# Keys times values of two neighbouring pairs of heads as one group of matmuls, and the queries' 576 columns divided 288 + 288

## The chip, the cores and the metric

The kernel runs on one core of one Trainium2 chip. Its time is the device time of one execution in microseconds (us). The kernel before took 711.76 us, the median of three runs (710.95 to 711.96).

## The reference

Linear attention over 8 batches, 8 heads, 576 positions and 64 dimensions, and then a feed-forward layer with the maximum of three products:

```python
q_s = np.exp(q - np.max(q, axis=-1, keepdims=True))
q_s = q_s / (np.sum(q_s, axis=-1, keepdims=True) + 1e-09)
k_s = np.exp(k - np.max(k, axis=2, keepdims=True))
k_s = k_s / (np.sum(k_s, axis=2, keepdims=True) + 1e-09)
kv = np.einsum('bhsd,bhse->bhde', k_s, v)
attn = np.einsum('bhsd,bhde->bhse', q_s, kv)
x = attn.transpose(0, 2, 1, 3).reshape(4608, 512)
h = np.maximum(np.maximum(x @ w1, x @ w2), x @ w3)   # w1..w3: 512 x 768
return h @ w_out                                     # 768 x 512
```

## The kernel before

**What is computed where.** The heads are worked on in pairs: 8 batches of 4 pairs are 32 pairs, numbered n = 4b + g, and a pair's 2 x 64 dimensions fill the 128 partitions. The feed-forward layer runs over nine chunks of 512 rows: chunk c below 8 holds the first 512 positions of batch c, and the ninth the last 64 positions of all eight batches (the tile `left`). Its products are made exact enough by splitting each operand into a high and a low part in the 32-bit format fp32r: x and the weights each become two tiles, and three matmuls (low weight by high x, high weight by low x, high by high) take the place of one. A gate's matmul (L775, into `pf`) and one of the second layer (L814, also `pf`) each stream 512 columns, with a weight load of 128 x 128 for each. "Wide matmul" stands for one of these below. There are 2592 of them.

**The attention of a pair.** The first two batches (8 pairs, "turned" in the code) go another way, which the change leaves alone. The other 24 pairs ("plain") run so:

- keys: the maximum over the positions by three DVE operations (L486 to L488) and a partition reduction on POOL (L491), then the subtraction on DVE (L494, into `ke`), then the exponential on ACT (L501). The tile `ke` has two buffers.
- keys times values (L519): ten matmuls of 65 columns (64 of the values and one of ones, which gives the sum), five slices of positions by two heads, each head into its own half of the partitions of `sm`. They are plain fp32, and the trace shows two matmul records for each. `sm` has one PSUM bank.
- normalization: 1/sum on DVE (L530, L531), the scaled product rounded to fp32r on ACT (L535, `bdh`) and the rest of it on DVE (L539, `bdl`), both as matrices of 128 x 128 with the heads' blocks on the diagonal.
- queries: softmax on DVE and ACT, then a transpose in blocks on DVE (L613, `tb`), eight DMAs on SP that put the blocks in place (L626, `qT`), and the split into `q_h` (ACT, L632) and `q_l` (DVE, L635).
- queries times keys-values (L690): three fp32r products (`bdh` by `q_l`, `bdl` by `q_h`, `bdh` by `q_h`) over 576 columns. Since a PSUM bank holds 512, each product is one matmul of 512 columns into `pa` and one of 64 into `sm`. `pa` has three banks, `pf` four.
- x: ACT rounds the result to its high part (L693 for the 512 columns, L700 for the 64), DVE subtracts for the low part (L695, L702).

**What sets the order.** Nothing is ordered by hand here: a planner (`Streams`) takes every piece of work as a `Step` with an engine, an estimated cost, what it waits for (`after`), the buffers that it takes and frees, and a rank. It issues the step that can begin first by its own clocks, and at equal time the one with the lowest rank. TensorE's gates and second-layer matmuls have the highest ranks and so fill what is left between the steps of the attention. The result is one fixed order for each engine; an engine works through its list in order, and waits on semaphores. SP's list holds all loads and the `qT` and output DMAs.

Of the kernel before, what the change touches and what calls it, by code (L numbers as in the profile page):

```python
# [43 lines left out]
BANKS = 3, 1  # L44

Q_BY_ACT = (0, 3, 4, 5, 6, 7)

Q_AFTER = (1,)


def dve(n):
    return (n + 90) / 960
# [150 lines left out]
def linear_attention_then_maxout_ffn(  # L203
# [63 lines left out]
    vbuf = [const.tile([P, 2, 5, NV], F32, name=f"vt{i}") for i in range(2)]  # L267
    bdh, bdl = [], []
    early = early_stack.enter_context(tc.tile_pool(name="early", bufs=1))
# [25 lines left out]
    nc.gpsimd.memset(bdf, 0.0)  # L295

    def main_rows(src, b, hs):
        return src[b, hs, 0:CH].rearrange("h (p s) d -> p h s d", s=4)
# [8 lines left out]
    for c in range(B + 1):  # L307
        in_pf += [(c, j, i) for j in range(NJ) for i in range(3)] + [(c, "y", t) for t in range(4)]
    st = Streams({"pf": 4, "pa": BANKS[0], "sm": BANKS[1], "keT": 1, "hp": NJ, "tmp": 3, "ke": 2, "qe": 2, "qf": 1, "qt": 2, "tb": 1, "qT": 2, "qhl": 1}, {"pf": in_pf})
    late_pools, turn_pools = [], []  # L310
# [67 lines left out]
    class Pair:  # L378


        def __init__(self, b, g):
            self.b, self.g = b, g
            self.hs = slice(2 * g, 2 * g + 2)
            self.n = b * NP + g
            self.m = self.n % 2
            self.turned = b < TURNED
            if b == 0:
                self.kt, self.vt, self.qt = k0[:, :, self.hs], v0[:, self.hs], q0[:, self.hs]
            else:
                self.kt, self.vt = kbuf[self.m], vbuf[self.m]  # L390
# [5 lines left out]
        def ago(self, what, *u):  # L396

            return (what, self.n - 2, *u) if self.n >= 2 else None

# [22 lines left out]
        def v_load(self):  # L422
            if self.b:
                prev = self.ago("kv") if self.n >= NP + 2 else None
# [55 lines left out]
        def k_plain(self):  # L480
# [10 lines left out]
            nc.gpsimd.partition_all_reduce(kma, km, P, bass_isa.ReduceOp.max)  # L491
            yield Step("V", dve(640), take=[("ke", n)], gives=("ksub", n), port="V")
            ke = self.ke = att.tile([P, 5, 2, D], F32, name="ke")
            nc.vector.tensor_tensor(  # L494
# [4 lines left out]
            )  # L499
            yield Step("A", act(640))  # L500
            nc.scalar.activation(out=ke, in_=ke, func=AF.Exp)  # L501

        def k_steps(self):
            n, turned = self.n, self.turned
            yield from self.k_turned() if turned else self.k_plain()
            ke = self.ke
            after = turned and n in Q_AFTER
            yield Step(
                "T", 0.9, [("v", n), None if turned else self.ago("xmm")], take=() if turned else [self.small_room()],
                free=[("ke", n)], gives=("kv", n),  # L510
            )
            if not turned:
                self.take_small()
            kv = self.sm[:, 2 * P : 3 * P]
            nv = D if turned else NV
            for s in range(5):
                rows = slice(0, LEFT if turned and s == 4 else P)
                for hh, r in enumerate(heads):
                    nc.tensor.matmul(  # L519
                        out=kv[r, :nv], lhsT=ke[rows, s, hh, :], rhs=self.vt[rows, hh, s, 0:nv],  # L520
                        start=(s == 0), stop=(s == 4),
                    )
            yield Step("V", 0.35)
            rk = att.tile([P, 1], F32, name="rk", bufs=4)
            if turned:
                nc.vector.tensor_scalar(
                    out=rk, in0=self.ks[:, 0:1], scalar1=self.ks[:, 1:2], scalar2=1e-9, op0=ALU.add, op1=ALU.add
                )
            else:
                nc.vector.tensor_scalar_add(out=rk, in0=kv[:, D:NV], scalar1=1e-9)  # L530
            nc.vector.reciprocal(out=rk, in_=rk)  # L531
            yield Step("A", 0.65, free=[self.small_room()] if turned and not after else (), gives=("bd", n) if turned else None)
            for r in heads:
                to = bdf[:, n] if turned else bdh[self.m]
                nc.scalar.activation(out=to[r, r], in_=kv[r, 0:D], func=AF.Copy, scale=rk[r])  # L535
            if not turned:
                yield Step("V", 0.45, gives=("bd", n))
                for r in heads:
                    nc.vector.scalar_tensor_tensor(  # L539
                        out=bdl[self.m][r, r],  # L540
                        in0=kv[r, 0:D],
                        scalar=rk[r],
                        in1=bdh[self.m][r, r].bitcast(F32),
                        op0=ALU.mult,
                        op1=ALU.subtract,
                    )


        def q_steps(self):
# [66 lines left out]
            for i in range(P // BL):  # L616
                for e in range(2):
                    end = i == P // BL - 1 and e == 1
                    yield Step(
                        "S", 0.6, take=[("qT", n)] if i == e == 0 else (), free=[("tb", n)] if end else (),  # L620
                        gives=("qT", n) if end else None, kb=36,
                    )
                    if i == e == 0:
# [4 lines left out]
                        in_=tb[BL * i : BL * (i + 1), e, :],  # L628
                    )
            yield Step("A", act(S), [("qT", n)], take=[("qhl", n)])  # L630
            q_h = turn_pools[0].tile([P, S], F32R, name="q_h", bufs=1)
# [38 lines left out]
        def x_steps(self):  # L670
            n, b = self.n, self.b
            room = ("pa", ("x", n))
            after_sums = self.turned and n in Q_AFTER
            cost = 0.5 if after_sums else f32(CH) if self.turned else 3 * f32r(CH) + 0.2
            freed = ("qe", ("xn", n)) if after_sums else ("qf" if self.turned else "qhl", n)
            after = [("bd", n), ("qhl", n), ("gates", b - 2) if b >= 2 else None, "late" if b == 1 else None]
            yield Step("T", cost, after, take=[room], gives=("xmm", n), free=[freed])
            xT = pa.tile([P, CH], F32, name="pa")
# [12 lines left out]
            h, lo = (xbuf[b % 2][:, i, self.g, :] for i in range(2))  # L691
            yield Step("A", act(CH))
            nc.scalar.copy(out=h, in_=xT)  # L693
            yield Step("V", dve(CH), free=[room], gives=("x", b, self.g))
            nc.vector.tensor_sub(out=lo, in0=xT, in1=h.bitcast(F32))  # L695
            if self.turned:
                return
            h, lo = (left[:, i, self.g, b * LEFT : (b + 1) * LEFT] for i in range(2))
            yield Step("A", act(LEFT))
            nc.scalar.copy(out=h, in_=self.sm[:, 0:LEFT])  # L700
            yield Step("V", dve(LEFT), free=[self.small_room()], gives=("xl", b, self.g))
            nc.vector.tensor_sub(out=lo, in0=self.sm[:, 0:LEFT], in1=h.bitcast(F32))  # L702

# [196 lines left out]
    def open_turn():  # L900
        yield Step("-", 0.0, [("split", n) for n in range(NS)] + [("x", 1, g) for g in range(NP)], gives="turn")
        start_stack.close()
        turn_pools.append(ctx.enter_context(tc.tile_pool(name="turn", bufs=1, side="right", reuse_waits="tile")))
        for i in range(2):
            nc.gpsimd.memset(kbuf[i][LEFT:P, :, 4, :], LOWEST)
            nc.gpsimd.memset(vbuf[i][:, :, :, D:NV], 1.0)
            nc.gpsimd.memset(vbuf[i][LEFT:P, :, 4, :], 0.0)
        for name, to in (("bdh", bdh), ("bdl", bdl)):
            for i in range(2):
                to.append(turn_pools[0].tile([P, P], F32R, name=f"{name}{i}"))  # L910
                nc.gpsimd.memset(to[i].bitcast(F32), 0.0)
# [97 lines left out]
```

## Time and profile before

| | |
|---|---|
| median of three runs | 711.76 us |
| profiled execution, first to last instruction | 711.8 us |
| wide matmuls of the gates (L775), on the chain | 63% of the span |
| wide matmuls of the second layer (L814), on the chain | 21% |
| keys times values (L519 into `sm`), on the chain | 3.0% |
| queries times keys-values (L690), on the chain | 3.6% into `pa`, 0.3% into `sm` |
| DVE, ACT, POOL busy | 56%, 34%, 8% |

In rows of a timeline the columns are the start (us), how long the instruction lasted (us), the engine, the line, the operation, what it writes and reads, and its shape; in square brackets stands the idle time of its engine just before it. PE is TensorE's matmul side and PEld its weight loads. A matmul's recorded length runs past the start of the next one, because matmuls are pipelined; what a matmul costs is read from one start to the next.

### The profile page before, as it was taken

To read this page: it belongs to the slowest core of one execution; us is meant where nothing else is said; L and a number is where in the kernel's file an instruction comes from. 1 tells how busy PE (TensorE), PEld (TensorE's weight loads), DVE (VectorE), ACT (ScalarE), POOL (GpSimd) and SP (SyncE) were. 2 spreads that over 40 slices of the span, in tenths; PEclk is the share of its full clock that TensorE was granted. 3 is DMA by queue.
4 is the path that set the end of the run, shared out by engine and by line. 5 is a ranking of instruction groups with operands and counts; after the bars stand their busy time and mean duration, and the time that the engine had idled before them with its cause. 6 is when DMAs were issued, how large, how long until landed. Compare 5 with 4: busy or idle time off the path is not lost.

```text
span 711.8 us, 9805 instructions
## 1 busy us (share of the span) xinstructions
PE 681.8 (96%) x3542; PEld 553.5 (78%) x3542; DVE 400.0 (56%) x804; ACT 245.0 (34%) x554; POOL 56.3 (8%) x71
## 2 busy tenths in 40 slices
PE   3579999999999999999999999999999999999997
PEld 2367777788887888888888888888888888888886
DVE  5679988789789775865576547643432112211220
ACT  5479867334343324312442134223321111111111
POOL 3223232200010001000000000000000000000000
PEclk9779999999999999999999999999999999999999
DMA  9747523344363215420342035302200010010002
GB/s 222 207 134 232 169 93 106 110 105 113 80 175 103 62 41 154 122 51 17 106 134 73 16 95 135 82 0 72 72 2 0 16 45 0 1 45 15 1 0 60
DMA packets 83280, 58.06 MB, mean 82 GB/s; under 512 B 49184, under 2 KB 74784, under 8 KB 83232
## 3 DMA queue, kind: packets, MB, share of 16 engines
q1 hardware_dynamic: 83152, 57.31, 28.9%
q8 instruction: 28, 0.46, 0.3%
q14 instruction: 20, 0.16, 0.1%
q10 hardware_dynamic: 80, 0.13, 0.0%
HBM read 40.89 MB, written 9.44 MB: 71 GB/s over the span
## 4 chain that ended last, share of the span: by engine, by line
PE 92%; DMA 3%; SPq 2%; DVE 1%; ACT 0%; issue 0%; ACTq 0%; DVEq 0%
PE pf L775 63%; PE pf L814 21%; PE pa L690 4%; DMA wst<-in_moe_w_dram 3%; PE sm L519 3%; SPq L870 0%; SPq L413 0%; PE sm L690 0%; PE pa L645 0%; PE pa L453 0%; PE pa L744 0%; SPq L873 0%; DVE qm L559 0%; DVE wl L374 0%; PE pa L472 0%
## 5 line engine op out<-in xcount | busy, mean ns | idle before, releaser
L775 PE MATMUL pf<-x,wh 128*128 128x512 f32 x1152 | 356.8, 391 | 0.0
L775 PEld LDWEIGHTS pf<-x,wh 128*128 128x128 f32 x1152 | 216.7, 188 | 45.2 <-issue 0.2
L775 PE MATMUL pf<-x,wl 128*128 128x512 f32 x576 | 229.8, 399 | 0.7 <-ACT bdf L535 0.7
L787 DVE TENSOR_TENSOR m<-pf,m 128x512 f32<-128x512 f32 x108 | 74.6, 690 | 179.0 <-PE pf L775 174.6
L775 PEld LDWEIGHTS pf<-x,wl 128*128 128x128 f32 x576 | 108.2, 188 | 25.3 <-ACT bdf L535 0.9
L790 ACT CAST h_h<-m 128x512 fp32r<-128x512 f32 x54 | 33.5, 621 | 201.5 <-DVE m L787 201.5
L814 PE MATMUL pf<-ol,h_h 128*128 128x512 f32 x216 | 88.1, 408 | 0.0
L814 PE MATMUL pf<-oh,h_l 128*128 128x512 f32 x216 | 84.4, 391 | 0.0
L814 PE MATMUL pf<-oh,h_h 128*128 128x512 f32 x216 | 84.1, 389 | 0.0
L784 ACT COPY m<-pf 128x512 f32<-128x512 f32 x54 | 31.6, 586 | 59.4 <-PE pf L775 59.1
L814 PEld LDWEIGHTS pf<-ol,h_h 128*128 128x128 f32 x216 | 40.5, 188 | 9.4 <-issue 0.7
L814 PEld LDWEIGHTS pf<-oh,h_l 128*128 128x128 f32 x216 | 40.5, 188 | 9.0
L794 DVE TENSOR_TENSOR h_l<-m,h_h 128x512 fp32r<-128x512 f32 x54 | 37.0, 686 | 18.0 <-ACT h_h L790 17.9
L814 PEld LDWEIGHTS pf<-oh,h_h 128*128 128x128 f32 x216 | 40.6, 188 | 8.4 <-issue 0.7
L491 POOL PARTITION_ALL_REDUCE kma<-km x24 | 17.3, 722 | 347.4 <-DVE ke L494 281.2
L775 PE MATMUL pf<-left,wh 128*128 128x512 f32 x144 | 44.4, 389 | 0.0
L832 ACT COPY m<-pf 128x512 f32<-128x512 f32 x35 | 20.5, 587 | 55.2 <-PE pf L814 54.9
L359 POOL TENSOR_TENSOR wst<-wx,wst 128x512 int32<-128x512 int32 x24 | 31.3, 1305 | 90.1 <-DVE wx L355 58.8
L695 DVE TENSOR_TENSOR x<-pa,x 128x512 fp32r<-128x512 f32 x32 | 22.0, 688 | 26.9 <-ACT x L693 26.8
L693 ACT CAST x<-pa 128x512 fp32r<-128x512 f32 x32 | 18.7, 584 | 39.5 <-PE sm L690 33.9
L775 PEld LDWEIGHTS pf<-left,wh 128*128 128x128 f32 x144 | 27.0, 188 | 5.7
L613 DVE STREAM_TRANSPOSE tb<-qt 128x576 f32<-128x576 f32 x24 | 30.6, 1275 | 1.2 <-DMA qT<-tb 0.9
(143 smaller groups left out, 675.3 us busy)
## 6 DMA issues: line engine op xcount, KB each, us to landing
wst<-in_moe_w_dram SPq DMA_DIRECT2D x18, 512.0 KB, 5.4
out_dram<-m SPq DMA_DIRECT2D x32, 256.0 KB, 2.5
vt<-in_v_dram SPq DMA_DIRECT2D x56, 128.0 KB, 3.0
qt<-in_q_dram SPq DMA_DIRECT2D x24, 288.0 KB, 3.1
qT<-tb SPq DMA_DIRECT2D x192, 36.0 KB, 1.9
kt<-in_k_dram SPq DMA_DIRECT2D x24, 256.0 KB, 3.1
wst<-in_moe_w_out_dram SPq DMA_DIRECT2D x6, 512.0 KB, 3.5
q<-in_q_dram SPq DMA_DIRECT2D x8, 256.0 KB, 6.0
```

Of the source, the lines that this page charges most:

```text
L359: nc.gpsimd.tensor_add(out=low.bitcast(I32), in0=x.bitcast(I32), in1=low.bitcast(I32))
L519: nc.tensor.matmul(out=kv[r, :nv], lhsT=ke[rows, s, hh, :], rhs=self.vt[rows, hh, s, 0:nv], start=(s == 0), stop=(s == 4),)
L613: nc.vector.transpose(out=tb.rearrange("p e (c s) -> p s e c", s=QS), in_=self.qt.rearrange("p s (e c) -> p s e c", e=2))
L690: nc.tensor.matmul(out=out, lhsT=l, rhs=r[:, cs], start=(i == 0), stop=(i == last))
L695: nc.vector.tensor_sub(out=lo, in0=xT, in1=h.bitcast(F32))
L775: nc.tensor.matmul(out=ps, lhsT=l[:, cc, js], rhs=r, start=(cc == 0 and t == 0), stop=(cc == NC - 1 and t == 2))
L784: nc.scalar.copy(out=m, in_=self.m.pop((j, 0)))
L787: nc.vector.tensor_max(out=m, in0=self.m.pop((j, i)), in1=m)
L790: nc.scalar.copy(out=h, in_=m)
L794: unit[e].tensor_sub(out=lo, in0=m, in1=h.bitcast(F32))
L814: nc.tensor.matmul(out=po, lhsT=l, rhs=r[:, j, :], start=(j == 0 and i == 0), stop=(j == NJ - 1 and i == 2))
L832: nc.scalar.copy(out=o, in_=po)
```

## The change

- **Keys times values.** For the plain pairs the planner's step for L519 is gone from the even pairs. The step of the odd pair (new function `two_products`) issues both pairs' ten matmuls one behind the other, into columns 0 to 64 and 128 to 192 of one bank of `pa`. It waits for both pairs' values and for the even pair's exponential, beside its own. One DVE operation adds the epsilon for both pairs, and one takes both reciprocals; the scaled copies stay as they were, pair by pair. The odd pair's keys get a tile of their own, `kep`, with one buffer.
- **Values.** `vbuf` has four buffers in place of two for the plain pairs; the two new ones are filled with their constants by four more POOL memsets.
- **Queries times keys-values.** The 576 columns are divided 288 + 288: one matmul into `pa`, one into a tile of `sm` that holds nothing else. The second half holds 224 columns of x and the 64 of `left`, so that ACT and DVE now each copy 288, 224 and 64 columns, where they copied 512 and 64.
- **The planner** is given the new costs (1.4 for the group, six times 288 columns for the product), the new buffers, and the order in which `tb` is handed out. The constant `X_F32` is False, so that `by_f32` is always false and its branches do nothing.

The core of the diff:

```diff
-    st = Streams({"pf": 4, "pa": BANKS[0], "sm": BANKS[1], "keT": 1, "hp": NJ, "tmp": 3, "ke": 2, "qe": 2, "qf": 1, "qt": 2, "tb": 1, "qT": 2, "qhl": 1}, {"pf": in_pf})
+    st = Streams({"pf": 4, "pa": BANKS[0], "sm": BANKS[1], "keT": 1, "hp": NJ, "tmp": 3, "ke": 2, "kep": 1, "qe": 2, "qf": 1, "qt": 2, "tb": 1, "qT": 2, "qhl": 1}, {"pf": in_pf, "tb": list(range(TURNED * NP, B * NP))})
...
+                    fresh = self.n < TURNED * NP + 4
+                    prev = ("turn" if self.n % 4 >= 2 else ("kv", self.n % 4 + 6)) if fresh else self.ago("kv", 4)
...
+                    if not self.turned:
+                        self.vt = vbuf[self.n % 4]
...
-            yield Step("A", act(640))
+            yield Step("A", act(640), gives=("kexp", n))
             nc.scalar.activation(out=ke, in_=ke, func=AF.Exp)
+            if n % 2:
+                yield from self.two_products()
+
+        def two_products(self):
+
+            n, both = self.n, (pairs[divmod(self.n - 1, NP)], self)
+            room = [("pa", ("kv", n))]
+            yield Step(
+                "T", 1.4, [("v", n - 1), ("v", n), ("kexp", n - 1), self.ago("xmm", 3), self.ago("xmm")], take=room,
+                free=[("ke", n - 1), ("kep", n)], gives=("kv", n),
+            )
+            kv = pa.tile([P, CH], F32, name="pa")
+            for i, p in enumerate(both):
+                for s in range(5):
+                    for hh, r in enumerate(heads):
+                        nc.tensor.matmul(
+                            out=kv[r, i * P : i * P + NV], lhsT=p.ke[:, s, hh, :], rhs=p.vt[:, hh, s, :],
+                            start=(s == 0), stop=(s == 4),
+                        )
+            yield Step("V", 0.35, gives=("kv", n - 1))
+            rk = att.tile([P, 2], F32, name="rk2", bufs=2)
+            nc.vector.tensor_scalar_add(out=rk, in0=kv.rearrange("p (i c) -> p i c", c=P)[:, 0:2, D], scalar1=1e-9)
+            nc.vector.reciprocal(out=rk, in_=rk)
+            for i, p in enumerate(both):
...
-            cost = 0.5 if after_sums else f32(CH) if self.turned else 3 * f32r(CH) + 0.2
+            cost = 0.5 if after_sums else f32(CH) if self.turned else 4 * f32r(S) if fine else 6 * f32r(S // 2)
...
-                parts = [(xT, slice(0, CH))] + ([] if self.turned else [(self.sm[:, 0:LEFT], slice(CH, S))])
+                half = S // 2
+                if self.turned:
+                    parts = [(xT, slice(0, CH))]
+                else:
+                    xT2 = sm.tile([P, CH], F32, name="sm")
+                    parts = [(xT[:, :half], slice(0, half)), (xT2[:, :half], slice(half, S))]
...
+            yield Step("A", act(half))
+            nc.scalar.copy(out=h[:, :half], in_=xT[:, :half])
+            yield Step("A", act(rest))
+            nc.scalar.copy(out=h[:, half:], in_=xT2[:, :rest])
...
+        vbuf.extend(turn_pools[0].tile([P, 2, 5, NV], F32, name=f"vt{i}") for i in (2, 3))
```

**What the planner makes of it.** The order of TensorE is the same in both up to the first group of keys times values of the plain pairs. Further on, in the chunks of the fourth and later batches, the same pattern returns for every pair of pairs. TensorE's list there, around a group of keys times values (`vt` are the values, `ke` and `kep` the exponentials; the `pf` rows are the second layer), before:

```order
L814 MATMUL pf<-ol,h_h 128x512
L814 MATMUL pf<-oh,h_h 128x512
L814 MATMUL pf<-oh,h_l 128x512
L519 MATMUL sm<-vt_93,ke 64x65 x10
L814 MATMUL pf<-ol,h_h 128x512
```

and changed:

```order
L874 MATMUL pf<-ol,h_h 128x512
L874 MATMUL pf<-oh,h_h 128x512
L874 MATMUL pf<-oh,h_l 128x512
L532 MATMUL pa<-vt_1370,ke 64x65 x10
L532 MATMUL pa<-vt_1371,kep 64x65 x10
L874 MATMUL pf<-ol,h_h 128x512
```

Two groups of ten now stand without a wide matmul between them, and there are 12 such places where there were 24. In this stretch the group stands 6 wide matmuls behind the last product of the queries and 15 ahead of the next; before, it was 15 ahead of the next as well. The very first group of plain pairs stands 21 wide matmuls later than before (the 403rd against the 382nd).

TensorE's list around a product of queries with keys-values (`bdh`, `bdl`), in the same stretch, before:

```order
L814 MATMUL pf<-oh,h_l 128x512
L690 MATMUL pa<-q_l,bdh_1378 128x512
L690 MATMUL sm<-q_l,bdh_1378 128x64
L690 MATMUL pa<-q_h,bdl_1382 128x512
L690 MATMUL sm<-q_h,bdl_1382 128x64
L690 MATMUL pa<-q_h,bdh_1378 128x512
L690 MATMUL sm<-q_h,bdh_1378 128x64
L814 MATMUL pf<-ol,h_h 128x512
```

and changed:

```order
L874 MATMUL pf<-oh,h_l 128x512
L741 MATMUL pa<-q_l,bdh_1382 128x288
L741 MATMUL sm<-q_l,bdh_1382 128x288
L741 MATMUL pa<-q_h,bdl_1386 128x288
L741 MATMUL sm<-q_h,bdl_1386 128x288
L741 MATMUL pa<-q_h,bdh_1382 128x288
L741 MATMUL sm<-q_h,bdh_1382 128x288
L874 MATMUL pf<-ol,h_h 128x512
```

Six matmuls stay six; only their columns differ, and no wide matmul stands among them.

DVE's list where the first group gets its second pair's keys (L494 before, L509 now, from `kt_91`), before:

```order
L613 STREAM_TRANSPOSE tb<-qt 128x9x64
L794 TENSOR_TENSOR h_l<-m,h_h 128x512
L530 TENSOR_SCALAR rk<-sm 128x1
L531 RECIPROCAL rk<-rk 128x1
L494 TENSOR_TENSOR ke<-kt_91,kma 128x2x5x64
L604 TENSOR_SCALAR qs_148<-qs_148 128x9
```

and changed:

```order
L654 STREAM_TRANSPOSE tb<-qt 128x9x64
L854 TENSOR_TENSOR h_l<-m,h_h 128x512
L509 TENSOR_TENSOR kep<-kt_91,kma 128x2x5x64
L645 TENSOR_SCALAR qs_148<-qs_148 128x9
L646 RECIPROCAL qs_148<-qs_148 128x9
L497 TENSOR_TENSOR kh<-kt_90 128x256
```

The subtraction of the second pair no longer stands behind the first pair's reciprocal, which waited for the first pair's matmuls.

More of the change, by code (lines that the diff above doesn't have):

```diff
@@ L48 @@
 Q_AFTER = (1,)
+X_F32 = False
 def dve(n):
@@ L267, in linear_attention_then_maxout_ffn @@
     vbuf = [const.tile([P, 2, 5, NV], F32, name=f"vt{i}") for i in range(2)]
-    bdh, bdl = [], []
+    bdh, bdl, bdf2 = [], [], []
     early = early_stack.enter_context(tc.tile_pool(name="early", bufs=1))
@@ L295, in linear_attention_then_maxout_ffn, with by_f32 @@
     nc.gpsimd.memset(bdf, 0.0)
+    def by_f32(n):
+        return X_F32 and n >= TURNED * NP
     def main_rows(src, b, hs):
@@ L389, in __init__ @@
             else:
-                self.kt, self.vt = kbuf[self.m], vbuf[self.m]
+                self.kt, self.vt = kbuf[self.m], vbuf[self.m] if self.turned else None
                 if self.turned:
@@ L394, in __init__, with ago @@
                     self.vt = self.vt.rearrange("p (h s d) -> p h s d", h=2, s=5)
-        def ago(self, what, *u):
-            return (what, self.n - 2, *u) if self.n >= 2 else None
+        def ago(self, what, back=2):
+            return (what, self.n - back) if self.n >= back else None
         def small_room(self):
@@ L423, in v_load @@
             if self.b:
-                prev = self.ago("kv") if self.n >= NP + 2 else None
+                if self.turned:
+                    prev = self.ago("kv") if self.n >= NP + 2 else None
+                else:
+                    fresh = self.n < TURNED * NP + 4
+                    prev = ("turn" if self.n % 4 >= 2 else ("kv", self.n % 4 + 6)) if fresh else self.ago("kv", 4)
                 for hh in range(2):
                     yield Step("S", 0.64, [prev], kb=128 if self.turned else 200)
+                    if not self.turned:
+                        self.vt = vbuf[self.n % 4]
                     nc.sync.dma_start(out=self.vt[:, hh, 0:4, 0:D], in_=head_rows(v, self.b, 2 * self.g + hh))
@@ L491, in k_plain @@
             nc.gpsimd.partition_all_reduce(kma, km, P, bass_isa.ReduceOp.max)
-            yield Step("V", dve(640), take=[("ke", n)], gives=("ksub", n), port="V")
-            ke = self.ke = att.tile([P, 5, 2, D], F32, name="ke")
+            room = ("kep" if n % 2 else "ke", n)
+            yield Step("V", dve(640), take=[room], gives=("ksub", n), port="V")
+            if n % 2:
+                ke = self.ke = turn_pools[0].tile([P, 5, 2, D], F32, name="kep", bufs=1)
+            else:
+                ke = self.ke = att.tile([P, 5, 2, D], F32, name="ke")
             nc.vector.tensor_tensor(
@@ L499, in k_plain @@
             )
-            yield Step("A", act(640))
+            yield Step("A", act(640), gives=("kexp", n))
             nc.scalar.activation(out=ke, in_=ke, func=AF.Exp)
-        def k_steps(self):
-            n, turned = self.n, self.turned
-            yield from self.k_turned() if turned else self.k_plain()
-            ke = self.ke
[L507 to L513, printed above, removed]
+            if n % 2:
+                yield from self.two_products()
@@ new lines, in two_products @@
+        def two_products(self):
[18 more added lines that the diff above has]
+            for i, p in enumerate(both):
+                fine = by_f32(p.n)
+                last = [] if i == 0 else room
+                yield Step("A", 0.65, gives=("bd", p.n) if fine else None, free=last if fine else ())
+                for r in heads:
+                    nc.scalar.activation(
+                        out=(bdf2 if fine else bdh)[p.m][r, r], in_=kv[r, i * P : i * P + D], func=AF.Copy,
+                        scale=rk[r, i : i + 1],
+                    )
+                if fine:
+                    continue
+                yield Step("V", 0.45, gives=("bd", p.n), free=last)
+                for r in heads:
+                    nc.vector.scalar_tensor_tensor(
+                        out=bdl[p.m][r, r],
+                        in0=kv[r, i * P : i * P + D],
+                        scalar=rk[r, i : i + 1],
+                        in1=bdh[p.m][r, r].bitcast(F32),
+                        op0=ALU.mult,
+                        op1=ALU.subtract,
+                    )
@@ L514, in k_steps @@
+        def k_steps(self):
+            n = self.n
+            if not self.turned:
+                yield from self.k_plain()
+                return
+            yield from self.k_turned()
+            ke = self.ke
+            after = n in Q_AFTER
+            yield Step("T", 0.9, [("v", n)], free=[("ke", n)], gives=("kv", n))
             kv = self.sm[:, 2 * P : 3 * P]
-            nv = D if turned else NV
             for s in range(5):
-                rows = slice(0, LEFT if turned and s == 4 else P)
+                rows = slice(0, LEFT if s == 4 else P)
@@ L518, in k_steps @@
                 for hh, r in enumerate(heads):
                     nc.tensor.matmul(
-                        out=kv[r, :nv], lhsT=ke[rows, s, hh, :], rhs=self.vt[rows, hh, s, 0:nv],
+                        out=kv[r, :D], lhsT=ke[rows, s, hh, :], rhs=self.vt[rows, hh, s, 0:D],
                         start=(s == 0), stop=(s == 4),
@@ L524, in k_steps @@
             rk = att.tile([P, 1], F32, name="rk", bufs=4)
[L525 to L530, printed above, removed]
+            nc.vector.tensor_scalar(
+                out=rk, in0=self.ks[:, 0:1], scalar1=self.ks[:, 1:2], scalar2=1e-9, op0=ALU.add, op1=ALU.add
+            )
             nc.vector.reciprocal(out=rk, in_=rk)
-            yield Step("A", 0.65, free=[self.small_room()] if turned and not after else (), gives=("bd", n) if turned else None)
+            yield Step("A", 0.65, free=() if after else [self.small_room()], gives=("bd", n))
             for r in heads:
[L534 to L546, printed above, removed]
+                nc.scalar.activation(out=bdf[r, n, r], in_=kv[r, 0:D], func=AF.Copy, scale=rk[r])
         def q_steps(self):
@@ L620, in q_steps @@
                         "S", 0.6, take=[("qT", n)] if i == e == 0 else (), free=[("tb", n)] if end else (),
-                        gives=("qT", n) if end else None, kb=36,
+                        gives=("qhl" if by_f32(n) else "qT", n) if end else None, kb=36,
                     )
@@ L629, in q_steps @@
                     )
+            if by_f32(n):
+                self.terms = [(bdf2[self.m], self.qT)]
+                return
             yield Step("A", act(S), [("qT", n)], take=[("qhl", n)])
@@ L673, in x_steps @@
             after_sums = self.turned and n in Q_AFTER
-            cost = 0.5 if after_sums else f32(CH) if self.turned else 3 * f32r(CH) + 0.2
-            freed = ("qe", ("xn", n)) if after_sums else ("qf" if self.turned else "qhl", n)
+            fine = by_f32(n)
+            cost = 0.5 if after_sums else f32(CH) if self.turned else 4 * f32r(S) if fine else 6 * f32r(S // 2)
+            freed = ("qe", ("xn", n)) if after_sums else ("qf" if self.turned else "qT" if fine else "qhl", n)
             after = [("bd", n), ("qhl", n), ("gates", b - 2) if b >= 2 else None, "late" if b == 1 else None]
-            yield Step("T", cost, after, take=[room], gives=("xmm", n), free=[freed])
+            small = ("sm", n)
+            yield Step("T", cost, after, take=[room] if self.turned else [room, small], gives=("xmm", n), free=[freed])
             xT = pa.tile([P, CH], F32, name="pa")
@@ L685, in x_steps @@
             else:
-                parts = [(xT, slice(0, CH))] + ([] if self.turned else [(self.sm[:, 0:LEFT], slice(CH, S))])
+                half = S // 2
+                if self.turned:
+                    parts = [(xT, slice(0, CH))]
+                else:
+                    xT2 = sm.tile([P, CH], F32, name="sm")
+                    parts = [(xT[:, :half], slice(0, half)), (xT2[:, :half], slice(half, S))]
                 last = len(self.terms) - 1
@@ L691, in x_steps @@
             h, lo = (xbuf[b % 2][:, i, self.g, :] for i in range(2))
[L692 to L695, printed above, removed]
             if self.turned:
+                yield Step("A", act(CH))
+                nc.scalar.copy(out=h, in_=xT)
+                yield Step("V", dve(CH), free=[room], gives=("x", b, self.g))
+                nc.vector.tensor_sub(out=lo, in0=xT, in1=h.bitcast(F32))
                 return
+            rest = CH - half
+            yield Step("A", act(half))
+            nc.scalar.copy(out=h[:, :half], in_=xT[:, :half])
+            yield Step("A", act(rest))
+            nc.scalar.copy(out=h[:, half:], in_=xT2[:, :rest])
+            yield Step("V", dve(half), free=[room])
+            nc.vector.tensor_sub(out=lo[:, :half], in0=xT[:, :half], in1=h[:, :half].bitcast(F32))
+            yield Step("V", dve(rest), gives=("x", b, self.g))
+            nc.vector.tensor_sub(out=lo[:, half:], in0=xT2[:, :rest], in1=h[:, half:].bitcast(F32))
             h, lo = (left[:, i, self.g, b * LEFT : (b + 1) * LEFT] for i in range(2))
             yield Step("A", act(LEFT))
-            nc.scalar.copy(out=h, in_=self.sm[:, 0:LEFT])
-            yield Step("V", dve(LEFT), free=[self.small_room()], gives=("xl", b, self.g))
-            nc.vector.tensor_sub(out=lo, in0=self.sm[:, 0:LEFT], in1=h.bitcast(F32))
+            nc.scalar.copy(out=h, in_=xT2[:, rest:half])
+            yield Step("V", dve(LEFT), free=[small], gives=("xl", b, self.g))
+            nc.vector.tensor_sub(out=lo, in0=xT2[:, rest:half], in1=h.bitcast(F32))
     def left_queries():
@@ L903, in open_turn @@
         turn_pools.append(ctx.enter_context(tc.tile_pool(name="turn", bufs=1, side="right", reuse_waits="tile")))
+        vbuf.extend(turn_pools[0].tile([P, 2, 5, NV], F32, name=f"vt{i}") for i in (2, 3))
         for i in range(2):
             nc.gpsimd.memset(kbuf[i][LEFT:P, :, 4, :], LOWEST)
+        for i in range(4):
             nc.gpsimd.memset(vbuf[i][:, :, :, D:NV], 1.0)
             nc.gpsimd.memset(vbuf[i][LEFT:P, :, 4, :], 0.0)
-        for name, to in (("bdh", bdh), ("bdl", bdl)):
+        for name, to in (("bdf", bdf2),) if X_F32 else (("bdh", bdh), ("bdl", bdl)):
             for i in range(2):
-                to.append(turn_pools[0].tile([P, P], F32R, name=f"{name}{i}"))
+                to.append(turn_pools[0].tile([P, P], F32 if X_F32 else F32R, name=f"{name}{i}"))
                 nc.gpsimd.memset(to[i].bitcast(F32), 0.0)
```

## The prediction

> **What bounds the kernel now.** I read four views: the page, the waits of TensorE, the windows, and the timeline around the places that the change touches. The page first:
>
> ```profile
> span 711.8 us, 9805 instructions
> PE 681.8 (96%) x3542; PEld 553.5 (78%) x3542; DVE 400.0 (56%) x804; ACT 245.0 (34%) x554; POOL 56.3 (8%) x71
> PE 92%; DMA 3%; SPq 2%; DVE 1%; ACT 0%; issue 0%; ACTq 0%; DVEq 0%
> ```
>
> TensorE is busy for 96% of the span, and 92% of the chain that ended last is its own work. The rest of the chain is loads at the start. The waits of TensorE's matmuls, longest and last of ten rows:
>
> ```profile
> PE pf L658 <- ACT qf L649: 6.5, 1, 6.5
> ...
> PE pa L681 <- DVE rk L526: 0.3, 1, 0.3
> ```
>
> None of the ten names the plain pairs' keys times values (L519 into `sm`) or a product with `q_l` or `q_h`; all lie in the first two batches, before 60 us. Where the changed work runs, the windows show the same (columns: window, its length, then busy us and count of each engine, granted clock, DMA share, GB/s):
>
> ```profile
> 141.00:160.00 19.00, 19.00 (x118) 15.27 (x117) 15.86 (x33) 6.90 (x13) 2.02 (x3) 1.00 0.40 103
> 160.00:208.00 48.00, 48.00 (x286) 38.81 (x283) 40.33 (x87) 19.20 (x41) 2.81 (x4) 1.00 0.41 112
> 337.00:376.00 39.00, 39.00 (x241) 31.47 (x241) 24.87 (x57) 15.54 (x33) 2.81 (x4) 1.00 0.43 119
> ```
>
> PE is busy without a gap at the full granted clock (1.00). So from here on every us that TensorE saves comes off the time, as long as the other engines keep up; DVE, at 40.33 of 48.00 us, is the next one. The price of a wide matmul, from the chain of waits:
>
> ```profile
> 625.69 16.32 PE pf L814 x72
> ```
>
> That is 16.32 / 72 = 0.227 us from start to start.
>
> **Keys times values.** One group and the wide matmuls around it, PE and then the weight loads, with the groups' means behind:
>
> ```profile
> 195.04 0.39 PE L814 MATMUL pf<-oh,h_h 128*128 128x512 f32 x1
> 195.26 0.39 PE L814 MATMUL pf<-oh,h_l 128*128 128x512 f32 x1
> 195.58 0.80 PE L519 MATMUL sm<-vt,ke 128*64 128x65 f32 x20
> 196.31 0.50 PE L814 MATMUL pf<-ol,h_h 128*128 128x512 f32 x1
> 196.65 0.40 PE L814 MATMUL pf<-oh,h_h 128*128 128x512 f32 x1
> ...
> 195.04 0.19 PEld L814 LDWEIGHTS pf<-oh,h_l 128*128 128x128 f32 x1
> 195.58 0.67 PEld L519 LDWEIGHTS sm<-vt,ke 128*64 128x64 f32 x20 [0.35 <-issue]
> ...
> L519 PE MATMUL sm<-vt,ke 128*64 128x65 f32 x480 | 19.3, 226 | 0.1
> L519 PEld LDWEIGHTS sm<-vt,ke 128*64 128x64 f32 x544 | 18.2, 137 | 10.2 <-issue 8.7 <-DVE wx L350 0.8 <-ACT m L784 0.4
> ```
>
> From 195.26 to 196.65 pass 1.39 us, and two of the starts in it are wide matmuls; less 2 x 0.227 the group costs 0.94 us. The twenty records themselves need less. By PE, 0.80 less one duration of 0.226 are 19 steps, 0.030 each, 0.60 for twenty; by the loads, 0.67 less 0.137 give 0.028 each, 0.56. I take 0.58. The other 0.36 us is paid once for each group, on the way in (0.32 from 195.26 to 195.58 where 0.227 is usual; the loader idles 0.35 without a releaser, and 8.7 us over 24 groups) and on the way out (0.34 from 196.31 to 196.65). The change leaves 12 such passages of 24 and adds no matmul: 12 x 0.36 = **4.3 us less**. Bounds: 4.6 with the loads' 0.56; nothing, if the step from the first pair's ten to the second's costs as much as the passage that it replaces. I take 4.3, since inside a group the records already pass from one head and slice to the next at 0.03.
>
> **Queries times keys-values.** One product, PE and then its loads:
>
> ```profile
> 201.00 0.39 PE L814 MATMUL pf<-oh,h_l 128*128 128x512 f32 x1
> 201.23 0.40 PE L690 MATMUL pa<-q_l,bdh 128*128 128x512 f32 x1
> 201.47 0.19 PE L690 MATMUL sm<-q_l,bdh 128*128 128x64 f32 x1
> 201.50 0.47 PE L690 MATMUL pa<-q_h,bdl 128*128 128x512 f32 x1
> 201.81 0.19 PE L690 MATMUL sm<-q_h,bdl 128*128 128x64 f32 x1
> 201.84 0.47 PE L690 MATMUL pa<-q_h,bdh 128*128 128x512 f32 x1
> 202.15 0.19 PE L690 MATMUL sm<-q_h,bdh 128*128 128x64 f32 x1
> 202.18 0.47 PE L814 MATMUL pf<-ol,h_h 128*128 128x512 f32 x1
> 202.49 0.39 PE L814 MATMUL pf<-oh,h_h 128*128 128x512 f32 x1
> ...
> 201.47 0.19 PEld L690 LDWEIGHTS pa<-q_h,bdl 128*128 128x128 f32 x1
> 201.58 0.19 PEld L690 LDWEIGHTS sm<-q_h,bdl 128*128 128x128 f32 x1
> ```
>
> From 201.00 to 202.49 pass 1.49 us with two wide starts in it: the six matmuls cost 1.49 - 0.454 = 1.036 us, 0.345 for each 512 + 64. The 512 behind a 64 starts only 0.03 after it, but the matmul behind that comes 0.31 later where 0.227 is usual: two loads of 128 x 128 follow each other at 0.11 (201.47, 201.58), and the 64 columns are too short to hide the next load. So 64 columns cost 0.115 here, most of it load. No row shows 288 columns. From below, a line through the starts (0.03 for 64, 0.227 for 512) gives 0.129; from above, a line through the costs (0.115 for 64, 0.227 for 512) gives 0.171, and six of these are 1.03: no gain at all. I take 0.13, since what makes the 64 dear is a load of 0.11, and that fits beneath 0.13:
>
> ```profile
> 296.30 1.73 PE pa L744 x16
> ```
>
> Here sixteen fp32 matmuls of 64 columns, each with a full load, pass at 0.108 each, so 0.11 is the pace of loads and no accident of one place. Six at 0.13 are 0.78, and 24 x (1.036 - 0.78) = **6.1 us less**. As an estimate by a page: the Trainium skill, "TensorE: Matmul & The Clock Gate", section "Back-to-back issue gap", gives an isolated step of N/2.4 + 2.5 ns, 122.5 ns for 288 columns; by it this term would be 7.2 us and the time 700.3. For 512 columns it gives 216 ns where the row above shows 227, so the trace is the dearer.
>
> **What else moves.** ACT and DVE copy 288 + 224 + 64 columns in place of 512 + 64:
>
> ```profile
> L693 ACT CAST x<-pa 128x512 fp32r<-128x512 f32 x32 | 18.7, 584 | 39.5 <-PE sm L690 33.9 <-PE pa L690 5.5
> L700 ACT CAST left<-sm 128x64 fp32r<-128x64 f32 x24 | 5.2, 216 | 0.0
> ```
>
> On a line between 216 and 584 ns, 288 columns take 0.40 and 224 take 0.35: ACT has 0.16 us more for each pair, 3.9 us over 24, with ACT at 19.20 of 48.00 us in its busiest window. DVE pays about the same for its three subtractions and wins it back with 24 short operations fewer on the sums. Both I cost at nothing; without the cover of wide matmuls it would be up to 0.3 us a pair. The four more memsets (0.12 to 0.20 us each) go to POOL, idle for 5.97 us before its first reduction:
>
> ```profile
> 135.68 0.48 POOL L918 PARTITION_ALL_REDUCE spare<-ones  x1 [5.97 <-issue]
> ```
>
> SP issues as many loads as before, but six value loads now stand among the four outputs, ahead of the first `qT`:
>
> ```profile
> 130.71 5.39 SPq L837 DMA_DIRECT2D out_dram<-m  x4
> 143.02 5.03 SPq L626 DMA_DIRECT2D qT<-tb  x8
> ```
>
> Six issues of some 0.6 us fit between 130.71 and 143.02.
>
> The added wait is the real risk: the group needs both pairs' exponentials, and behind it in TensorE's list stands every wide matmul.
>
> ```profile
> 141.64 0.34 PE L519 MATMUL sm<-vt,ke 128*64 128x65 f32 x4
> 144.72 0.74 ACT L501 ACTIVATE ke<-ke 128x640 f32<-128x640 f32 x1
> 345.87 0.58 DVE L539 SCALAR_TENSOR_TENSOR bdl<-sm,rk,bdh 64x64 fp32r<-64x64 f32 x2
> 348.18 0.40 PE L690 MATMUL pa<-q_l,bdh 128*128 128x512 f32 x1
> ```
>
> The first group ran at 141.64, and the second pair's exponential ended at 145.46. The new order puts the group 21 wide matmuls later, at 146.4: 0.9 us to spare, and DVE's list brings the subtraction forward. In the later stretch `bdl` ended at 346.45 and its product began at 348.18, with 1.73 us to spare; the new order keeps 15 wide matmuls between them and puts a subtraction of keys in between as before, and one short operation of 0.2. I cost the waits at nothing.
>
> **Sum:** 711.8 - 4.3 - 6.1 = **701.4 us**. The profiled execution's span, 711.8, is the median of the runs (711.76) to 0.1, so nothing is converted.
>
> **Rivals.**
> 1. *288 columns cost what the upper line says* (0.171): only the groups gain, 707.5. For it: each product alternates `bdh` and `bdl` and loads anew for all six. Against it: the 0.108 of sixteen loads in a row. Chance 0.10.
> 2. *The passage isn't saved*, because the second pair's operands start the passage anew: 705.7. Against it: nothing but the addresses changes between the two tens. 0.06.
> 3. *New waits.* The planner's order leaves less room: if the first group is 1.5 us late and the eight products up to 240 us lose 0.2 each, 3.1 us return, 704.5. For it: DVE at 40.33 of 48.00. Against it: not one wait in the old order, made by the same rules. 0.13.
> 4. *Slower: loads that don't hide under short matmuls.* If a load and 288 columns follow each other, a step is 0.11 + 0.13 = 0.24, six are 1.44, and 24 x 0.40 = 9.7 are lost: 717.2. It is slower by over 0.2% from 0.21 a step on. Against it: a wide step of 0.227 holds a load that begins with it (both at 195.04), so loads hide under 512 columns. 0.03. The Trainium skill has this rule, in the same page, section "The mechanism": a weight load overlaps a running matmul only where the row groups differ, and all six here use all 128 rows. By that rule, the wide rows would be at 0.34 too, and the trace shows 0.227.
> 5. *More than summed*: 0.123 a step, or cheaper passages, 699 to 700.4. 0.06.
>
> That the change doesn't do what it says is excluded by the order: the groups stand together and the shapes are 288.
>
> **How the numbers follow.** The forecast has 0.62, with 700.4 to 702.9 of its own (the 0.3 us of the loads' bound and 0.7 for 0.125 a step below, 1.5 us of small waits above). The range of 700.0 to 706.0 takes in rivals 2 and 3 and half of 5; it leaves out 1, 4 and the tails, some 0.18. What a measurement of this kernel can tell from no change is about 0.2%, 1.4 us. Faster by more than that: all but 4 and a remnant of 1 in which the step goes beyond the load's recorded 0.19 (709.7 or more): 0.94. Within it 0.03, slower 0.03.
>
> **What would show it.** Right: PE's waits stay empty after 141 us; a group of forty records costs some 1.52 us from wide to wide instead of twice 0.94; starts of 288 columns follow at 0.13, and the six cost 0.78. Wrong: starts at 0.17 or more (rival 1, 4), a second pair's ten that begin with 0.3 of idle loader (2), or rows of waits at L532 or L741 (3). A wait at the first group for `kep`, or at the products of the third batch for `q_l`, would be where the order is tightest.

## The result, and the profile after

The changed kernel takes **703.84 us** (median of four runs, 703.14 to 704.30); the kernel before took 711.86 us beside it (710.95 to 712.46). The ratio is 0.9887 with a 95% interval of [0.9873, 0.9901]: 8.0 us less. 701.4 us was predicted, with a range of 700.0 to 706.0. The profiled execution has a span of 702.2 us and took 704.3 us. A run's time is thus some 2 us above its span, also for the kernel before: in a later set of runs its median was 711.97 us, in an execution with a span of 710.2.

The page of the changed kernel, by the lines that were shown for the kernel before:

```profile
span 702.2 us, 9785 instructions
PE 675.4 (96%) x3542; PEld 551.7 (79%) x3542; DVE 398.5 (57%) x804; ACT 249.1 (35%) x578; POOL 58.5 (8%) x75
PE 93%; DMA 2%; SPq 1%; DVE 1%; ACT 1%; issue 0%; ACTq 0%; DVEq 0%
```

TensorE is still the bound, and it still waits for nothing after the first 60 us: the view of its waits has no row from there to the end. ACT has 24 copies more than before and 4.1 us more of work. The same windows as before:

```profile
141.00:160.00 19.00, 19.00 (x120) 15.46 (x119) 14.41 (x32) 7.12 (x15) 1.06 (x1) 1.00 0.45 117
160.00:208.00 48.00, 48.00 (x287) 39.62 (x286) 41.97 (x92) 20.92 (x46) 5.66 (x7) 1.00 0.49 130
```

PE is without a gap, and DVE has come a little nearer (41.97 of 48.00 us). The group and the product on PE's timeline:

```profile
343.24 0.39 PE L874 MATMUL pf<-oh,h_h 128*128 128x512 f32 x1
343.47 0.40 PE L874 MATMUL pf<-oh,h_l 128*128 128x512 f32 x1
343.80 0.80 PE L532 MATMUL pa<-vt,ke 128*64 128x65 f32 x20
344.43 0.75 PE L532 MATMUL pa<-vt,kep 128*64 128x65 f32 x20
345.12 0.50 PE L874 MATMUL pf<-ol,h_h 128*128 128x512 f32 x1
345.45 0.39 PE L874 MATMUL pf<-oh,h_h 128*128 128x512 f32 x1
...
348.43 0.39 PE L874 MATMUL pf<-oh,h_l 128*128 128x512 f32 x1
348.65 0.30 PE L741 MATMUL pa<-q_l,bdh 128*128 128x288 f32 x1
348.79 0.30 PE L741 MATMUL sm<-q_l,bdh 128*128 128x288 f32 x1
348.92 0.30 PE L741 MATMUL pa<-q_h,bdl 128*128 128x288 f32 x1
349.05 0.29 PE L741 MATMUL sm<-q_h,bdl 128*128 128x288 f32 x1
349.18 0.30 PE L741 MATMUL pa<-q_h,bdh 128*128 128x288 f32 x1
349.32 0.30 PE L741 MATMUL sm<-q_h,bdh 128*128 128x288 f32 x1
349.45 0.39 PE L874 MATMUL pf<-ol,h_h 128*128 128x512 f32 x1
349.69 0.40 PE L874 MATMUL pf<-oh,h_h 128*128 128x512 f32 x1
```

The group of two pairs: 345.45 - 343.47 = 1.98 us, less two wide starts of 0.227 it is 1.53 us, where two groups cost 1.88. The product: 349.69 - 348.43 = 1.26, less 0.454 it is 0.81 us, where it cost 1.036. All 12 groups cost 1.52 or 1.53 us, and the 24 products 0.79 to 0.81. So the groups save 12 x 0.35 = 4.2 us and the products 24 x 0.23 = 5.5 us. Together that is 9.7 us, and only 8.0 came. What is lacking is found in instructions that the change does not touch. The chain at the end, all wide matmuls of the seventh batch's second layer, of the eighth batch's gates and second layer, and of the last chunk's gates, before and then changed:

```profile
559.89 16.36 PE pf L814 x72
576.25 49.44 PE pf L775 x216
625.69 16.32 PE pf L814 x72
642.01 48.97 PE pf L775 x216
```

```profile
549.61 16.33 PE pf L874 x72
565.94 50.20 PE pf L835 x216
616.14 16.33 PE pf L874 x72
632.47 48.97 PE pf L835 x216
```

The columns are start, time on the chain, and count. Three of the four rows are the same within 0.03 us. The gates of chunk 7 take 50.20 us in place of 49.44: 232.4 ns a step in place of 228.9, with the same instructions. Even before, they were slower than the 226.7 ns of the last chunk. Chunk 7 is odd, and the odd chunks stream x from the tile `x1`, the even ones from `x0`. Chunk 7 alone loses 0.76 us, which would make 3.0 us for the four odd chunks. The traces bear this out: among the gates' steps after 60 us, without the long ones (over 250 ns) beside groups, products and transposes, those of the odd chunks went from 229.1 to 232.6 ns (849 steps), which is 3.0 us more. Those of the even chunks went from 227.8 to 227.3 (791 steps), 0.4 us less. The expectations below go by a smaller figure, 230.0 to 233.1 ns over 612 steps and 1.9 us.

With 3.0 and 0.4 the sum closes: 9.7 - 3.0 + 0.4 is 7.1 us, and from the first gate of chunk 1 (at 131.94 us before, 129.55 changed) to the start of the last matmul pass 575.02 us before and 567.83 changed, 7.2 less. The difference from the 8.0 of the times lies ahead of chunk 1 or between executions; the ten profiled executions of this case begin chunk 1 at 128.8 to 131.9 us. The stretch from chunk 1's first gate to the last matmul is called "the stretch" below.

In the built program `x1` begins at byte 158912 of each partition before, and at 158976 in the changed kernel, since the two small tiles `rk2` lie ahead of it and take 32 bytes each. `x0` (90496) and all the gates' weights have not moved; each of them begins 384 bytes above a multiple of 512. Counted within 256 bytes, `x0` is thus 0 bytes away from the weights, and `x1` 64 before and 128 in the changed kernel. **Theory P** (place): the step of a matmul depends on where the streamed tile lies against the weights. **Rival O** (order): the gates are slower because of what ACT and DVE now do beside them.

### The profile page after: what moved, and what is told of

It reads as the page before. It is cut to its first block, busy times and chain, and to the rows that moved or that the text cites. A ratio compares the mean times of both kernels' runs of the same rounds, so it can differ in the third digit from the quotient of the medians.

```text
span 702.2 us, 9785 instructions
## 1 busy us (share of the span) xinstructions
PE 675.4 (96%) x3542; PEld 551.7 (79%) x3542; DVE 398.5 (57%) x804; ACT 249.1 (35%) x578; POOL 58.5 (8%) x75
## 4 chain that ended last, share of the span: by engine, by line
PE 93%; DMA 2%; SPq 1%; DVE 1%; ACT 1%; issue 0%; ACTq 0%; DVEq 0%
PE pf L835 64%; PE pf L874 21%; DMA wst<-in_moe_w_dram 2%; PE pa L532 2%; PE pa L741 2%; PE sm L741 1%; PE sm L575 0%; SPq L930 0%; PE pa L464 0%; PE pa L703 0%; PE pa L689 0%; SPq L418 0%; PE pa L804 0%; SPq L933 0%; DVE wl L379 0%
## 5 line engine op out<-in xcount | busy, mean ns | idle before, releaser
L835 PE MATMUL pf<-x,wl 128*128 128x512 f32 x576 | 229.1, 398 | 0.7 <-ACT bdf L587 0.7
L874 PE MATMUL pf<-ol,h_h 128*128 128x512 f32 x216 | 86.2, 399 | 0.0
L502 POOL PARTITION_ALL_REDUCE kma<-km x24 | 19.0, 793 | 281.3 <-DVE km L499 131.0
L835 PE MATMUL pf<-left,wl 128*128 128x512 f32 x72 | 28.0, 389 | 0.0
L679 DVE TENSOR_TENSOR q_l<-qT,q_h 128x576 fp32r<-128x576 f32 x24 | 18.1, 754 | 16.6 <-ACT q_h L676 15.9
```

Source lines behind the costliest of these rows:

```text
L679: nc.vector.tensor_sub(out=q_l, in0=self.qT, in1=q_h.bitcast(F32))
L835: nc.tensor.matmul(out=ps, lhsT=l[:, cc, js], rhs=r, start=(cc == 0 and t == 0), stop=(cc == NC - 1 and t == 2))
L874: nc.tensor.matmul(out=po, lhsT=l, rhs=r[:, j, :], start=(j == 0 and i == 0), stop=(j == NJ - 1 and i == 2))
```

## The experiments

Four kernels first, on one chip; the kernel before had a median of 711.97 us there.

**The shift undone (`a_no_shift`).** The changed kernel, with the new tile in the slots of the old one:

```diff
-            rk = att.tile([P, 2], F32, name="rk2", bufs=2)
+            rk = att.tile([P, 2], F32, name="rk", bufs=4)
...
-            rk = att.tile([P, 1], F32, name="rk", bufs=4)
+            rk = att.tile([P, 2], F32, name="rk", bufs=4)[:, 0:1]
```

> The changed kernel, with the two small tiles of the group's reciprocals put into the slots that the turned pairs' reciprocals have, so that the tiles behind them (h_h, h_l, m, x1, oh, ol) lie where they lay before the change, 64 bytes lower than in the changed kernel; instructions and shapes are the same. Theory P (place): the gates of the odd chunks, which stream x1, cost 233.1 ns from wide to wide in the changed kernel because x1 moved; they return to the 230.0 ns of before, 612 steps x 3 ns = 1.9 us less than the changed kernel, about 702.0 us. Rival O (order): they are slower because of what ACT and DVE now do beside them; they stay at 233 ns and the time at 703.8 us.

702.09 us (702.01 to 702.46), ratio to before 0.9860 [0.9847, 0.9873]. That is 1.8 us less than the changed kernel, and the stretch takes 564.87 us, 3.0 less. The row of chunk 7 is back:

```profile
564.42 49.44 PE pf L835 x216
```

**The shift alone (`b_shift64`).** The kernel before, with `x1` at 158976:

```diff
-            rk = att.tile([P, 1], F32, name="rk", bufs=4)
+            rk = att.tile([P, 1], F32, name="rk", bufs=6)
```

> The kernel before, with two more buffers of the small reciprocals, so that h_h, h_l, m, x1, oh and ol lie 64 bytes higher, as in the changed kernel; nothing else differs. Theory P: the odd chunks' gates go from 230.0 to about 233 ns, the time from 711.9 to about 713.8 us. Rival O: no change, 711.9 us.

713.36 us (712.72 to 714.83), ratio 1.0018 [1.0010, 1.0027]:

```profile
576.79 50.20 PE pf L775 x216
```

64 bytes of unused space make the kernel before slower by 1.4 us, and chunk 7 takes the 50.20 us of the changed kernel. O would leave both kernels as they were, so it falls. The stretch takes 577.90 us, 2.9 more than before. So the place costs 2.9 to 3.0 us by the profiled executions, and 1.4 to 1.8 by the medians of the times; why the times show less was not settled.

**Further along (`c_align`).** The changed kernel, with `x1` at 159104, 128 bytes higher:

```diff
-            rk = att.tile([P, 2], F32, name="rk2", bufs=2)
+            rk = att.tile([P, 2], F32, name="rk2", bufs=6)
```

> The changed kernel, with four more buffers of 32 bytes, so that x1 lies 128 bytes higher, at 384 above a multiple of 512 bytes, where x0 and all the gates' weights lie too; h_h, h_l, oh and ol move along together. Theory P in its sharper form (the step is shortest where the streamed tile and the weights have the same place within 512 bytes): the odd chunks' gates go from 233.1 to the even ones' 227 to 229 ns, some 3 us less than the changed kernel, about 700.8 us. P in a loose form (only the 64 bytes did it): some value between 227 and 233. Rival O: 703.8 us.

**699.16 us** (698.28 to 701.39), ratio 0.9823 [0.9804, 0.9841], better than expected:

```profile
561.15 48.96 PE pf L835 x216
```

That is 226.7 ns a step, as in the last chunk. Over the 849 steps the odd chunks' gates went from 232.6 to 227.0 ns, 4.8 us; the time fell by 4.7 us from the changed kernel, and the stretch by 5.3 to 562.53. The even chunks' gates, whose tile did not move, stayed at 227.3 and 227.2 ns. Here is chunk 6 in the changed kernel and then in `c_align`:

```profile
500.60 49.01 PE pf L835 x216
```

```profile
495.87 48.96 PE pf L835 x216
```

This version beats both kernels, with the same instructions as the changed one.

**The groups alone (`d_group_only`).** The changed kernel, with 512 + 64 columns again (and with ACT's and DVE's copies of these shapes):

```diff
-                    parts = [(xT[:, :half], slice(0, half)), (xT2[:, :half], slice(half, S))]
+                    parts = [(xT[:, :CH], slice(0, CH)), (xT2[:, :LEFT], slice(CH, S))]
```

> The changed kernel with the queries' columns divided 512 + 64 as before: only the groups of two pairs are new. The prediction's sum: the six matmuls cost 1.04 us again, the group 1.54 us for two pairs, so 4.3 us less than before by the groups; less some 1.9 us that the 64 bytes take by theory P: 709.5 us (707.6 us by rival O). If the passages were not what the groups save, 711.9 us or more.

708.29 us (707.48 to 710.01), ratio 0.9949 [0.9935, 0.9963]. That is 3.7 us less than before, where 2.4 were expected with the place's 1.9; the interval, 707.3 to 709.3, just misses the expected 709.5 and takes in the 707.6 of rival O. By its time alone this run would thus side with O. But the chunk-7 row is 50.20 us again, so the place acts here too, and the stretch takes 573.05 us, 1.97 less than before; by the rows, 4.2 less for the groups and 3.0 more for the place would make it 1.2. The group on PE's timeline:

```profile
346.08 0.39 PE L869 MATMUL pf<-oh,h_l 128*128 128x512 f32 x1
346.40 0.80 PE L532 MATMUL pa<-vt,ke 128*64 128x65 f32 x20
347.03 0.76 PE L532 MATMUL pa<-vt,kep 128*64 128x65 f32 x20
347.71 0.50 PE L869 MATMUL pf<-ol,h_h 128*128 128x512 f32 x1
348.05 0.40 PE L869 MATMUL pf<-oh,h_h 128*128 128x512 f32 x1
```

348.05 - 346.08 - 0.454 = 1.52 us, as in the changed kernel. Why the time fell by 1.3 us more than expected was not settled.

Then four more, again beside the kernel before (711.78 us); the last three have a single time each.

**The columns alone (`e_288_only`).** The kernel before, pair by pair, with the product divided (and with ACT's and DVE's copies of these shapes):

```diff
-            kv = self.sm[:, 2 * P : 3 * P]
+            kv = self.sm[:, 2 * P : 3 * P] if turned else self.sm[:, 3 * P : 4 * P]
...
-                parts = [(xT, slice(0, CH))] + ([] if self.turned else [(self.sm[:, 0:LEFT], slice(CH, S))])
+                half = S // 2
+                parts = [(xT, slice(0, CH))] if self.turned else [(xT[:, :half], slice(0, half)), (self.sm[:, :half], slice(half, S))]
```

> The kernel before with the queries' columns divided 288 + 288; keys times values stay pair by pair in 24 groups (in columns 384 to 448 of the sm bank, behind the 288 of the product), and x1 lies where it lay before. By the sum, with a step as measured in the changed kernel (0.133 in place of the 0.13 predicted): the six matmuls cost 0.80 us in place of 1.04, and with the somewhat slower wide ones behind them 24 x 0.22 = 5.3 us less than before, 706.7 us. With theory P the four ways add up: before 712.0, groups -4.3, columns -5.3, place +1.9. If instead the two parts of the change needed each other, this one alone would give less than 4 us.

706.74 us (705.00 to 707.67), ratio 0.9928 [0.9911, 0.9945]: 5.0 us less, close to the expected 5.3; the stretch takes 569.47 us, 5.55 less. The two parts of the change add up, about: 3.7 and 5.0 are 8.7 by the times, and 1.97 and 5.55 are 7.5 by the stretch. Since `d_group_only` bears the shift of `x1` and `e_288_only` does not, these sums have the price of the place in them once, as has the changed kernel with its 8.0 and 7.2.

**Other shares (`f_384_192`).** `c_align` with 384 + 192 columns:

```diff
-                half = S // 2
+                half = 384
```

> The aligned version of the changed kernel (c_align) with the columns divided 384 + 192. What made the 64 columns dear? Theory L (the weight load's pace of 0.11 sets the least step): 384 columns take 0.173, 192 take the load's 0.11, a pair 0.28 where 288 + 288 take 0.266, six 0.85. Rival S (an fp32r matmul of few columns is slow in itself, four times per column as plain fp32 is): 192 columns take 0.32, six cost 1.5. Rival U (a straight line from 0.115 at 64 columns to 0.227 at 512): 192 take 0.147 and 384 take 0.195, six 1.03.

701.41 us. PE's timeline:

```profile
347.84 0.33 PE L741 MATMUL pa<-q_l,bdh 128*128 128x384 f32 x1
348.01 0.25 PE L741 MATMUL sm<-q_l,bdh 128*128 128x192 f32 x1
348.10 0.36 PE L741 MATMUL pa<-q_h,bdl 128*128 128x384 f32 x1
348.30 0.25 PE L741 MATMUL sm<-q_h,bdl 128*128 128x192 f32 x1
348.39 0.36 PE L741 MATMUL pa<-q_h,bdh 128*128 128x384 f32 x1
348.59 0.25 PE L741 MATMUL sm<-q_h,bdh 128*128 128x192 f32 x1
```

A pair costs 0.29 us (348.10 to 348.39), by the rule of the load's pace 0.28, by a slow short matmul 0.49, by a straight line 0.34. So 192 columns are billed at some 0.11, the pace of the loads: two weight loads around them start at 348.31 and 348.42. The 192 columns show 0.09 of it on their own step; the other part shows on the 384 behind them, which take 0.20 instead of 0.17.

**What the place is measured against (`g_256`, `h_all_shift`).** The first moves `x1` another 256 bytes on (`rk2` with 14 buffers, 159360). The second is `c_align` with a tile of 64 bytes ahead of everything, so that all other tiles, weights, `x0`, `x1` and `left` among them, move together:

```diff
+    pad = const.tile([P, 16], F32, name="pad")
+    nc.gpsimd.memset(pad, 0.0)
     wh = [const.tile([P, NC, DF], F32R, name=f"wh{i}") for i in range(3)]
```

> The changed kernel with 12 more buffers of 32 bytes: x1 lies at 128 above a multiple of 512 bytes, 256 away from the place of the gates' weights (384). Theory P with the places of the two operands compared within 512 bytes: the odd chunks' gates are slow, 229 to 234 ns. With the places compared within 256 bytes, or with x1's own place within 256 bytes as the cause (128 is that of x0 too): 227 to 228 ns as in c_align.

> c_align with a tile of 64 bytes ahead of everything, so that the gates' weights, x0, x1 and left all lie 64 bytes higher and their distances stay. Theory P by distance: all gates as in c_align, 227 to 228 ns, even and odd. By own place (what counts is where the streamed tile itself lies, 448 above a multiple of 512 now): even, odd and left chunks all change together, to some value from 229 to 233 ns, 4 us or more in sum.

699.66 and 699.14 us. Chunk 7 and the last chunk in `g_256`, then in `h_all_shift`:

```profile
562.54 48.96 PE pf L835 x216
...
627.82 48.96 PE pf L835 x216
```

```profile
562.01 48.96 PE pf L837 x216
...
627.29 48.96 PE pf L837 x216
```

256 bytes more change nothing, and 64 bytes for all tiles change nothing. So it is not `x1`'s own place that counts but its distance, within 256 bytes, from something that did not move with it in the first three runs. The tiles `h_h`, `h_l` and `m`, which ACT and DVE write beside the gates, did move with `x1`, and the last chunk's gates, which have the same writes beside them but stream `left`, take 48.96 or 48.97 us in all ten profiles. The gates read their weights besides, and of what is read or written in SBUF beside chunk 7's gates only these stayed in place. So the distance that counts is the one between the streamed tile and the weights. Three distances were measured for this matmul: 0 bytes (226.7 ns), 64 (228.9, the kernel before) and 128 (232.4, the changed kernel). Why it acts was not tried.

## Why the prediction was right, point by point

- **TensorE as the bound, and no new waits** (rival 3): right. No matmul of TensorE waits after the first 60 us, so none at a group or at a product of a plain pair. The tightest place, the first group, had more room than the 0.9 us that was estimated: `kep`'s exponential ended at 142.30 us and the group began at 144.27. (By the traces 351 wide matmuls of the gates and the second layer ran ahead of it, and 330 before; the difference is the 21 of the prediction.)

```profile
141.56 0.74 ACT L516 ACTIVATE kep<-kep 128x640 f32<-128x640 f32 x1
...
144.27 0.51 PE L532 MATMUL pa<-vt,ke 128*64 128x65 f32 x10
```

- **The groups, 4.3 us**: right in mechanism and size. A group of two pairs costs 1.53 us where 1.52 was forecast, and the second ten begin without a passage (344.43, 0.63 behind the first's 343.80). Rival 2 falls.
- **The products, 6.1 us**: right in mechanism, somewhat too large. A step of 288 columns takes 0.133 us and not 0.13 (348.79 to 349.32 are four steps): the line through the two starts had taken 0.03 for 64 columns as the price of their streaming, and left out most of a fixed part that the wide step shows too. 0.227 for 512 and 0.133 for 288 give 0.42 ns a column and some 0.012 us for each matmul. By the same rows the term is 5.5 us. The step of 0.133 rules out rivals 1 (0.171) and 4 (0.24), and `f_384_192` shows that the reason given for 0.13, the load's pace of 0.11, holds.
- **"Adds no matmul", the rest at nothing**: this is the step that failed: some 3.0 us went here by the traces (1.8 by the time of `a_no_shift`) that the sum did not have. No instruction was added to TensorE, and ACT, DVE, POOL and SP did hide their parts, but a new tile of 32 bytes in two buffers moved `x1`, and every wide matmul of the odd chunks got dearer. The prediction read all wide matmuls at 0.227 and did not look at whether they are equal; the row of 49.44 us for 216 steps (0.229) stood in the profile of before.
- **"Nothing is converted"**: the base of 711.8 us was right by luck. The times hold some 2 us beyond the span, and the profiled execution of before had a late start (first gate at 43.87 us, and at 41.51 in the changed kernel, long ahead of the first changed step). So its span was about as long as the median of the times, and the two errors cancelled.

```profile
43.87 0.77 PE L775 MATMUL pf<-x,wl 128*128 128x512 f32 x1
```

```profile
41.51 0.76 PE L835 MATMUL pf<-x,wl 128*128 128x512 f32 x1
```

By the measured terms, 711.86 - 4.2 - 5.5 + 3.0 - 0.4 is 704.8, and 703.84 was measured; the 0.9 us between them was not settled.

- **The range**: partly luck. 703.84 lies above the forecast's own 700.4 to 702.9. It lies in the part of the range that was there for rivals 2 and 3, and neither of them came; what brought it there, the place of `x1`, was on no list.

## What to carry to other kernels

Where TensorE is the bound, add up the passages and the steps from start to start, not the recorded lengths: few columns are billed at the pace of the next weight load, so dividing 576 as 288 + 288 beats 512 + 64 with the same count of matmuls. After any change, compare the steps of the matmuls that it did not touch; if they moved, look at where the tiles lie, since a small tile can shift large ones. Here 128 bytes of padding were worth as much as one of the two parts of the change (4.7 us).

## What the runs showed of the hardware that was not expected

- The step of an fp32r matmul of 128 x 512 with a load of 128 x 128 depends on the distance of the two operands in the partition: 226.7 ns at 0 bytes and at 256, 228.9 at 64 and 232.4 at 128 (chunk 7's rows).
- The passage of 0.36 us does not come with plain fp32 between fp32r matmuls as such; the groups' shape of 64 weight columns may be what brings it. Four fp32 transposes with full loads, among the changed kernel's gates:

```profile
64.46 0.62 PE L835 MATMUL pf<-x,wh 128*128 128x512 f32 x2
64.92 0.60 PE L689 MATMUL pa<-ident,qe 128*128 128x128 f32 x4
65.27 0.47 PE L835 MATMUL pf<-x,wl 128*128 128x512 f32 x1
65.59 0.62 PE L835 MATMUL pf<-x,wh 128*128 128x512 f32 x2
```

From 64.92 to 65.59 pass 0.67 us, four at the load's 0.11 and one wide step of 0.227; there is no passage. The Trainium skill, "TensorEngine Tiling (Array Packing)", section "Key Properties", says that a change of the tiling mode drains TensorE. That fits: the tens have 64 columns of weights, the transposes 128. No kernel here changed the shape alone, so this is not shown.
